# An RWKV-7 recurrence and its MLP on one core: the MLP's products as two of 64x128 in place of four of 64x64, and a planner without the count of instruction blocks

## The chip, the core and the metric

The kernel runs on one core of a Trainium2 chip. The metric is the device time of one execution in microseconds (us). A core has a matrix engine (TensorE; its matmuls are PE in the profile and its weight loads PEld), a vector engine (VectorE, DVE), a scalar engine (ScalarE, ACT), GpSimd (POOL) and a queue engine that starts DMAs here (SyncE, SP). Products are written to PSUM, from which ACT or DVE copies them to SBUF.

## The reference

Two blocks follow each other. The first is a recurrence over 768 time steps for 4 batches of 8 heads of 40 channels; the second is an MLP on the 3072 rows that come out of it.

```python
for t in range(S):                          # S = 768
    y[:, :, t] = einsum('bhd,bhde->bhe', r_t, state)
    Sa = einsum('bhde,bhe->bhd', state, a_t)
    state = state * w_t[:, :, None, :] - einsum('bhd,bhe->bhde', Sa, b_t)
    state = state + einsum('bhd,bhe->bhde', v_t, k_t)
x = y.transpose(0, 2, 1, 3).reshape(3072, 320)
h = x @ w_in                                # 320 x 2048
g = h * (1 / (1 + exp(-1.702 * h)))
out = g @ w_out                             # 2048 x 320
```

## The kernel before

The recurrence is computed in chunks of 64 time steps. There are 12 chunks; a chunk is two units (a pair of batches each), so there are 24 units. For each unit, products of 64 by 64 build the matrices that couple the steps of a chunk (prep, with the tiles ps_turn, ps_N, ps_A, ps_Av and ps_RV), six levels of doubling solve the triangular system (level, line 592, tile ps_level, each level in two halves b), the state goes on to the next chunk (update, ps_Z), and the output of the unit is read, scaled and turned (read, decayed, bridge: ps_y, y, x, ps_xT). All operands are 32-bit floats. TensorE runs each such product as two passes, each a weight load and a matmul. Four products run side by side on the four 64x64 quarters of the array: HALF chooses the rows or columns 0 to 63 or 64 to 127, and QUARTERS (line 191) lists the four combinations.

The MLP of a chunk j takes xT(j), 256 rows with the 320 channels in 5 slices of 64 for each of two row halves. `up` (line 731) makes ps_up for each of 8 blocks m of 256 hidden columns, in 5 parts, one for each slice k; ACT applies the gelu and writes g. `down` (line 748) makes ps_down for each of two halves p of the rows in 8 parts, each with two hidden slices f; ACT and DVE add the two PSUM banks into ob, and SP stores it. In both, r chooses the half of the rows of the array (the contraction) and the PSUM bank.

What order the instructions have is decided by a list scheduler in the kernel itself (Plan, line 56). Every task has a rank, a cost on each engine that can run it, what it reads and writes, the slots of each buffer, and possibly a pair of PSUM banks. There are four such pairs; tasks with `most=2` (the MLP's) may together hold two of them, and begin a new one only when two are clear. Recurrence tasks of unit i have ranks around 10 i, the conversion of the weights from 64-bit floats has ranks from 5000, and the MLP from 10000, so an MLP part is taken when nothing of a lower rank is ready. `order` goes through time: it takes for a free engine the first ready task by rank. The instructions of each engine are then issued in that order, and an engine runs them in order.

Buffers have a fixed number of slots: four for xT, ten for g, three for W (the levels' matrices). The bridge of chunk c writes xT(c) and so must come after up(c-4). Two of xT's slots hold raw weights at first.

The planner also counts TensorE's instructions. `pe` (line 225) gives a task its TensorE time and its number of instructions, 16 for each four products. `order` keeps how many were issued and when the present block of 256 began; `fetched` (line 112) lets a block begin no sooner than 3750 ns after the one before. Where the first ready TensorE task would so be held more than 100 ns, another ready one that would not be is taken in its place, if there is one:

```python
if took and e == "PE" and wait(took) > 100.0:
    took = next((t for t in able if e in t.engines and fits(t) and wait(t) <= 100.0), took)
```

Of the kernel before, what the change touches and what calls it, by code (L numbers as in the profile page):

```python
# [47 lines left out]

class Task:
    def __init__(self, rank, engines, fn, pair, most, size):  # L50
        self.instr = engines.pop("instr", 0)
        self.rank, self.engines, self.fn, self.pair, self.most, self.size = rank, engines, fn, pair, most, size
        self.after, self.then = set(), []


class Plan:

    BLOCK, FETCH = 256, 3750.0
    DELAY = {"PE": 330.0, "DVE": 130.0, "ACT": 130.0, "POOL": 150.0, "SP": 100.0}
    ISSUE = 60.0

# [27 lines left out]
    def order(self):  # L92
        for n, t in enumerate(self.tasks):
            t.n, t.left, t.ready = n, len(t.after), 0.0
            for o in t.after:
                o.then.append(t)
        free = dict.fromkeys(("PE", "ACT", "DVE", "POOL", "SP"), 0.0)
        pairs = [0.0] * self.pairs
        held, users = {}, {k: len(v) for k, v in self.of_pair.items()}
        coming = [(0.0, t.n) for t in self.tasks if not t.left]  # L100
        heapq.heapify(coming)
        able, now, wire, out, many = [], 0.0, 0.0, [], set()

        def fits(t):
            if t.pair is None or t.pair in held:
                return True
            clear = sum(p <= now for p in pairs)
            return clear > 0 if t.most is None else clear > 1 and len(many) < t.most

        issued, begun = 0, 0.0  # L110

        def fetched(t, start):

            at, left, ns, block = start, t.instr, t.engines["PE"] / t.instr, begun
            room = self.BLOCK - issued % self.BLOCK
            while left >= room:
                at += room * ns
                left -= room
                at = block = max(at, block + self.FETCH)
                room = self.BLOCK  # L120
            return at + left * ns, block

        def wait(t):
            return fetched(t, now)[0] - now - t.engines["PE"]

        while coming or able:
            while coming and coming[0][0] <= now:
                able.append(self.tasks[heapq.heappop(coming)[1]])
            able.sort(key=lambda t: (t.rank, t.n))
            took = None  # L130
            for e in free:
                if free[e] <= now:
                    took = next((t for t in able if e in t.engines and fits(t)), None)
                    if took and e == "PE" and wait(took) > 100.0:

                        took = next((t for t in able if e in t.engines and fits(t) and wait(t) <= 100.0), took)
                    if took:
                        break
            if not took:
                later = [x for x in (*free.values(), *pairs) if now < x < float("inf")]  # L140
                now = min(later + ([coming[0][0]] if coming else []))
                continue
            t = took
            able.remove(t)
            t.engine = e
            end = now + t.engines[e]
            if e == "PE":
                end, begun = fetched(t, now)
                issued += t.instr
            free[e] = end  # L150
            if e == "SP":
                wire = max(wire, now + 1500.0) + t.size / 170.0
                end = wire
            if t.pair is not None:
                if t.pair not in held:
                    held[t.pair] = next(i for i, p in enumerate(pairs) if p <= now)
                    pairs[held[t.pair]] = float("inf")
                    if t.most is not None:
                        many.add(t.pair)
                t.bank = held[t.pair]  # L160
                users[t.pair] -= 1
                if not users[t.pair]:
                    many.discard(t.pair)
                    pairs[t.bank] = end + self.DELAY[e]
            for o in t.then:
                o.ready = max(o.ready, end + (0.0 if o.engines.keys() == {e} else self.DELAY[e]))
                o.left -= 1
                if not o.left:
                    heapq.heappush(coming, (o.ready, o.n))
            t.start = now  # L170
            out.append(t)
        assert len(out) == len(self.tasks)
        return out
# [3 lines left out]
def rwkv7_gelu_quick(ctx: ExitStack, tc: tile.TileContext, time_d, w_d, chan_d, w_in, w_out, out):  # L177
    nc = tc.nc
    H, D, S = 8, 40, out.shape[0] // 4
    DM = H * D  # L180
# [5 lines left out]
    NM = NF // 2  # L186
    NK = DM // 64
    LEVELS = 6
    HALF = [slice(0, 64), slice(64, 128)]
    BITS = (0, 1)  # L190
    QUARTERS = [(0, 0), (1, 1), (0, 1), (1, 0)]
# [11 lines left out]
    def single(name, shape):  # L203
        return const.tile(shape, FP32, tag=name, name=name)

    def buf(name, n, shape, dt=FP32):

        if (name, n) not in tiles:
            s = n % plan.slots[name]
            tiles[name, n] = work.tile(shape, dt, tag=f"{name}{s}", name=name)  # L210
        return tiles[name, n]

    def psum(t, name):
        if t.pair not in psums:
            psums[t.pair] = banks.tile([128, 2, 512], FP32, tag=f"pair{t.bank}", name=name)
        return psums[t.pair]
# [7 lines left out]

    def pe(*sets):

        return {"PE": sum(n * 2 * max(58.0, cols / 1.2 + 3) for n, cols in sets), "instr": sum(16 * n for n, _ in sets)}

    def dve(n):
        return {"DVE": 170.0 + 1.03 * n}  # L230
# [1 line left out]
    def act(n):  # L232
        return {"ACT": 210.0 + 0.76 * n}
# [62 lines left out]
    w_in_sb = single("w_in_sb", [128, NK, NM, 128])  # L296
# [431 lines left out]
    g_of = lambda n: buf("g", n, [128, 2, 256])  # L728
    ob_of = lambda n: buf("ob", n, [128, DM])

    def up(j):
        for m in range(NM):
            n = j * NM + m

            def part(k, m=m):
                def go(t):
                    ph = psum(t, "ps_up")
                    for r, h in QUARTERS:
                        nc.tensor.matmul(ph[HALF[h], r, :256], w_in_sb[HALF[r], k, m, h * 64:(h + 1) * 64],  # L739
                                         xT_of(j)[HALF[r], k, :], start=k == 0, stop=k == NK - 1)  # L740
                return go
            for k in range(NK):
                plan.add(10000 + 100 * j + m, pe((1, 256)), part(k), reads=[("xT", j), ("w_in", (m // 2, k))], room=[("g", n)],
                         pair=("up", n), most=2)
            plan.add(10000 + 100 * j + m, act(512), lambda t, n=n: nc.scalar.activation(  # L745
                g_of(n), psum(t, "")[:, :, :256], ACT.Gelu_apprx_sigmoid), writes=[("g", n)], pair=("up", n))

    def down(j):
        for p in range(2):
            n = 2 * j + p  # L750

            def part(m, p=p, n=n):
                def go(t):
                    po = psum(t, "ps_down")
                    for f in (2 * m, 2 * m + 1):
                        for r, b in QUARTERS:
                            o = p * 128 + b * 64
                            nc.tensor.matmul(po[HALF[b], r, :DM], g_of(j * NM + m)[HALF[r], f % 2, o:o + 64],  # L758
                                             w_out_sb[HALF[r], f, :], start=f == 0, stop=f == NF - 1)
                return go  # L760
            for m in range(NM):
                plan.add(10000 + 100 * j + 20 * (p + 1) + m, pe((2, 320)), part(m),
                         reads=[("g", j * NM + m), ("w_out", 2 * m), ("w_out", 2 * m + 1)], pair=("down", n), most=2)

            def one(t, n=n):
                copy(t.engine)(ob_of(n), psum(t, "")[:, 0, :DM])  # L766

            def both(t, n=n):
                nc.vector.tensor_add(ob_of(n), ob_of(n), psum(t, "")[:, 1, :DM])  # L769

            def store(t, n=n, p=p):
                for b in BITS:
                    o = (2 * p + b) * S + j * C
                    nc.sync.dma_start(out[o:o + C, :], ob_of(n)[HALF[b]])
            plan.add(10000 + 100 * j, any2(320), one, writes=[("ob", n)], pair=("down", n))
            plan.add(10000 + 100 * j, dve(320), both, reads=[("ob", n)], writes=[("out", n)], pair=("down", n))
            plan.add(-100, {"SP": 120.0}, store, reads=[("ob", n), ("out", n)], size=128 * DM * 4)
# [77 lines left out]
```

## Time and profile before

| what | us |
|---|---|
| median of three runs | 1111.91 |
| lowest and highest run | 1109.09, 1114.43 |
| the profiled execution, whole | 1109.09 |
| the profiled execution, its span in the trace | 1107.4 |
| TensorE matmuls, busy | 912.8 |
| of it ps_level, all forms (L219) | 353.5 |
| of it ps_up (L739) | 251.7 |
| of it ps_down (L758) | 232.8 |
| ACT busy | 366.4 |
| DVE busy | 319.1 |

The page cuts the span into 40 slices; each digit is the busy share of an engine in tenths (9 is 90% or more):

```profile
PE   7566787756887777987768988688988999999998
DVE  4686666322423224123132131320231200000000
ACT  4333433443335333243342344333244221111211
PEclk8998989999999999999999999999999999999999
```

A slice is 27.7 us. The clock that the throttle granted to TensorE is near full throughout (mean 0.978). Weight loads overlap the matmuls. Busy times of matmuls overlap too where products run side by side; a group's busy time is the time in which at least one of its members runs.

### The profile page before, as it was taken

How to read it: one execution, taken by the hardware profiler on the slowest of the kernel's cores; microseconds unless marked ns; L12 is line 12 of the kernel's file. 1: busy time of each engine (PE TensorE's matmuls, PEld its weight loads, DVE VectorE, ACT ScalarE, POOL GpSimd, SP SyncE). 2: the span in 40 equal slices, each digit the busy share in tenths (PEclk: the TensorE clock that was granted, in tenths of full speed). 3: DMA queues.
4: the chain of work that ended last, by engine and by line, in shares of the span. 5: the costliest groups of instructions: out<-in, count | busy, mean ns of one | idle time of the engine just before them, and what ended most of it. 6: DMA issues, size and time to landing. Idle time of an engine off the chain costs nothing.

```text
span 1107.4 us, 67140 instructions
## 1 busy us (share of the span) xinstructions
PE 912.8 (82%) x32416; PEld 754.1 (68%) x32416; DVE 319.1 (29%) x688; ACT 366.4 (33%) x663; POOL 81.5 (7%) x115
## 2 busy tenths in 40 slices
PE   7566787756887777987768988688988999999998
PEld 6556676656676666777667867677877866666664
DVE  4686666322423224123132131320231200000000
ACT  4333433443335333243342344333244221111211
POOL 3322322100000000000010010000010000000000
PEclk8998989999999999999999999999999999999999
DMA  6333433201211011011111111201100000000000
GB/s 204 109 105 85 134 105 95 65 4 53 70 54 54 21 53 65 27 48 59 53 46 35 47 59 34 65 17 40 58 4 10 4 14 14 14 8 8 15 14 13
DMA packets 22542, 54.89 MB, mean 50 GB/s; under 512 B 2816, under 2 KB 14080, under 8 KB 22272
## 3 DMA queue, kind: packets, MB, share of 16 engines
q1 hardware_dynamic: 22272, 50.61, 14.8%
q8 instruction: 253, 4.15, 1.6%
q14 instruction: 17, 0.14, 0.0%
HBM read 46.66 MB, written 3.93 MB: 46 GB/s over the span
## 4 chain that ended last, share of the span: by engine, by line
PE 79%; issue 16%; DVE 2%; ACT 1%; DMA 0%; POOL 0%; SPq 0%; DVEq 0%; POOLq 0%; ACTq 0%
PE ps_up L739 19%; PE ps_down L758 19%; PE ps_level L219 18%; PE ps_turn L219 3%; PE ps_cum L219 2%; PE ps_y L219 2%; PE ps_N L219 2%; PE ps_Z L219 2%; PE ps_xT L219 1%; PE ps_saT L219 1%; PE ps_RV L219 1%; PE ps_Av L219 1%; PE ps_M L219 1%; PE ps_A L219 1%; PE ps_rz L219 1%
## 5 line engine op out<-in xcount | busy, mean ns | idle before, releaser
L219 PE MATMUL ps_level<-W 64*64 64x64 f32 (+2 forms) x8448 | 232.3, 236 | 61.3 <-issue 56.5
L219 PEld LDWEIGHTS ps_level<-W 64*64 64x64 f32 x8448 | 215.5, 137 | 77.4 <-issue 65.6
L739 PE MATMUL ps_up<-xT,w_in_sb 64*64 64x256 f32 x3840 | 251.7, 382 | 19.3 <-issue 17.2
L758 PE MATMUL ps_down<-w_out_sb,g 64*64 64x320 f32 x3072 | 232.8, 433 | 4.3 <-issue 4.1
L613 ACT COPY W<-ps_level 128x672 f32<-128x672 f32 (+1 forms) x220 | 148.7, 684 | 220.7 <-PE ps_level L219 214.2
L739 PEld LDWEIGHTS ps_up<-xT,w_in_sb 64*64 64x64 f32 x3840 | 160.5, 135 | 68.4 <-issue 28.6
L758 PEld LDWEIGHTS ps_down<-w_out_sb,g 64*64 64x64 f32 x3072 | 129.8, 134 | 70.4 <-issue 10.1
L219 PE MATMUL ps_level<-W,ident 64*64 64x80 f32 x2304 | 121.2, 238 | 8.2 <-issue 8.2
L745 ACT ACTIVATE g<-ps_up 128x512 f32<-128x512 f32 x96 | 57.4, 598 | 127.4 <-PE ps_up L739 126.4
L219 PEld LDWEIGHTS ps_level<-W,ident 64*64 64x64 f32 x2304 | 87.6, 138 | 10.2 <-issue 10.2
L769 DVE TENSOR_TENSOR ob<-ob,ps_down 128x320 f32<-128x320 f32 x24 | 11.7, 488 | 211.0 <-ACT ob L766 211.0
L766 ACT COPY ob<-ps_down 128x320 f32<-128x320 f32 x24 | 10.2, 426 | 127.5 <-PE ps_down L758 127.5
L330 POOL TENSOR_SCALAR scale<-scale 128x256 f32<-128x256 f32 (+1 forms) x36 | 41.3, 1160 | 116.0 <-DVE scale L326 116.0
L468 POOL TENSOR_TENSOR ah<-in_time,F 128x320 f32<-128x320 f32 x14 | 12.7, 904 | 360.5 <-ACT F L416 347.8
L473 POOL TENSOR_TENSOR kh<-in_time,G 128x320 f32<-128x320 f32 x18 | 16.6, 922 | 243.9 <-ACT G L414 146.2
L219 PE MATMUL ps_y<-kh,RV 64*64 64x40 f32 x768 | 28.8, 232 | 4.8 <-issue 4.8
L219 PE MATMUL ps_y<-bh,M 64*64 64x40 f32 x768 | 29.0, 235 | 4.0 <-issue 3.7
L613 DVE COPY W<-ps_level 128x416 f32<-128x416 f32 (+1 forms) x20 | 14.1, 709 | 63.1 <-PE ps_level L219 63.1
L219 PEld LDWEIGHTS ps_y<-kh,RV 64*64 64x64 f32 x768 | 27.4, 144 | 6.4 <-issue 5.2
L219 PE MATMUL ps_Z<-sa,bh 64*64 64x40 f32 x704 | 26.0, 226 | 4.1 <-issue 4.1
L219 PEld LDWEIGHTS ps_y<-bh,M 64*64 64x64 f32 x768 | 25.9, 145 | 4.6 <-issue 4.2
L508 DVE TENSOR_TENSOR W<-ps_N,upper 128x512 f32<-128x512 f32 x24 | 16.6, 691 | 42.7 <-PE ps_N L219 42.5
(113 smaller groups left out, 1111.8 us busy)
## 6 DMA issues: line engine op xcount, KB each, us to landing
in_time<-in_time SPq DMA_DIRECT2D x24, 800.0 KB, 4.6
in_chan<-in_chan SPq DMA_DIRECT2D x24, 512.0 KB, 4.3
raw<-in_w_in SPq DMA_DIRECT2D x40, 128.0 KB, 3.6
raw<-in_w_out SPq DMA_DIRECT2D x16, 320.0 KB, 3.7
in_w<-in_w SPq DMA_DIRECT2D x24, 160.0 KB, 3.4
out<-ob SPq DMA_DIRECT2D x48, 80.0 KB, 2.1
```

What stands on the lines that cost most here:

```text
L219: nc.tensor.matmul(o, lhsT, rhs, start=start, stop=True, skip_group_check=True)
L330: nc.gpsimd.tensor_scalar(scale().bitcast(FP32), scale().bitcast(FP32), low, high, ALU.max, ALU.min)
L468: plan.add(R, {"DVE": 490.0, "POOL": 900.0}, lambda t: of(t.engine).tensor_mul(ah[:, :, :D], by_head(in_time(i)[:, 3]), by_head(F_of(i))), ...
L473: plan.add(R, {"DVE": 490.0, "POOL": 900.0}, lambda t: of(t.engine).tensor_mul(kh[:, :, :D], by_head(in_time(i)[:, 0]), G()), reads=T("in_ ...
L508: plan.add(R + 1, dve(512), lambda t: nc.vector.tensor_tensor(W_of(6 * i).rearrange("p e b f n -> p e (b f) n")[:, :, :, o:o + 64], psum(t ...
L613: copy(t.engine)(W_of(s + 1)[:, :, b, :, lo:], view[:, :, :, lo:])
L739: nc.tensor.matmul(ph[HALF[h], r, :256], w_in_sb[HALF[r], k, m, h * 64:(h + 1) * 64], xT_of(j)[HALF[r], k, :], start=k == 0, stop=k == NK - 1)
L745: plan.add(10000 + 100 * j + m, act(512), lambda t, n=n: nc.scalar.activation(g_of(n), psum(t, "")[:, :, :256], ACT.Gelu_apprx_sigmoid), w ...
L758: nc.tensor.matmul(po[HALF[b], r, :DM], g_of(j * NM + m)[HALF[r], f % 2, o:o + 64], w_out_sb[HALF[r], f, :], start=f == 0, stop=f == NF - 1)
L766: copy(t.engine)(ob_of(n), psum(t, "")[:, 0, :DM])
L769: nc.vector.tensor_add(ob_of(n), ob_of(n), psum(t, "")[:, 1, :DM])
```

## The change

Two things change. The MLP's products use all 128 columns of the array at once: in `up` and `down` the loop over four quarters becomes a loop over the two row halves, with a stationary operand of 64x128 in place of 64x64, so that a part has two products of 128 output rows in place of four of 64. And the planner's count of instructions goes, with the rule that was built on it: a TensorE task takes its cost in time, and the first ready task by rank is taken.

```diff
 class Task:
     def __init__(self, rank, engines, fn, pair, most, size):
-        self.instr = engines.pop("instr", 0)
...
-    BLOCK, FETCH = 256, 3750.0
...
-        issued, begun = 0, 0.0
-
-        def fetched(t, start):
-
-            at, left, ns, block = start, t.instr, t.engines["PE"] / t.instr, begun
-            room = self.BLOCK - issued % self.BLOCK
-            while left >= room:
-                at += room * ns
-                left -= room
-                at = block = max(at, block + self.FETCH)
-                room = self.BLOCK
-            return at + left * ns, block
-
-        def wait(t):
-            return fetched(t, now)[0] - now - t.engines["PE"]
...
-                    if took and e == "PE" and wait(took) > 100.0:
-
-                        took = next((t for t in able if e in t.engines and fits(t) and wait(t) <= 100.0), took)
...
             end = now + t.engines[e]
-            if e == "PE":
-                end, begun = fetched(t, now)
-                issued += t.instr
             free[e] = end
...
-        return {"PE": sum(n * 2 * max(58.0, cols / 1.2 + 3) for n, cols in sets), "instr": sum(16 * n for n, _ in sets)}
+        return {"PE": sum(n * 2 * max(58.0, cols / 1.2 + 3) for n, cols in sets)}
...
                     ph = psum(t, "ps_up")
-                    for r, h in QUARTERS:
-                        nc.tensor.matmul(ph[HALF[h], r, :256], w_in_sb[HALF[r], k, m, h * 64:(h + 1) * 64],
+                    for r in BITS:
+                        nc.tensor.matmul(ph[:, r, :256], w_in_sb[HALF[r], k, m, :],
                                          xT_of(j)[HALF[r], k, :], start=k == 0, stop=k == NK - 1)
...
                     for f in (2 * m, 2 * m + 1):
-                        for r, b in QUARTERS:
-                            o = p * 128 + b * 64
-                            nc.tensor.matmul(po[HALF[b], r, :DM], g_of(j * NM + m)[HALF[r], f % 2, o:o + 64],
+                        for r in BITS:
+                            nc.tensor.matmul(po[:, r, :DM], g_of(j * NM + m)[HALF[r], f % 2, p * 128:p * 128 + 128],
                                              w_out_sb[HALF[r], f, :], start=f == 0, stop=f == NF - 1)
```

## The prediction

> **What bounds the kernel now.** I began with the page: how busy each engine is, and the DMA queues.
>
> ```profile
> span 1107.4 us, 67140 instructions
> PE 912.8 (82%) x32416; PEld 754.1 (68%) x32416; DVE 319.1 (29%) x688; ACT 366.4 (33%) x663; POOL 81.5 (7%) x115
> ...
> q8 instruction: 253, 4.15, 1.6%
> ```
>
> TensorE is the only engine that is busy more than a third of the time. It has 32416 matmuls and as many weight loads, 64832 instructions. The queue named "instruction" moved 253 packets and 4.15 MB: one packet for 64832 / 253 = 256 TensorE instructions, 16.4 KB each. So TensorE's program is fetched in blocks of 256 while it runs. The DMA view of two stretches gives the rate:
>
> ```profile
> q8 instruction: 129, 2.11, 1.8%
> ```
>
> That is 300 to 800 us: 129 blocks in 500 us, 3.88 us a block.
>
> ```profile
> q8 instruction: 19, 0.31, 0.9%
> ```
>
> That is 950 to 1100 us: 19 blocks in 150 us, 7.9 us a block. The two stretches have different limits. The timeline of TensorE shows the second:
>
> ```profile
> 946.32 1.34 PE L219 MATMUL ps_xT<-ident,x 64*64 64x64 f32 x80
> 947.48 17.41 PE L758 MATMUL ps_down<-w_out_sb,g 64*64 64x320 f32 x256
> 964.71 17.45 PE L739 MATMUL ps_up<-xT,w_in_sb 64*64 64x256 f32 x320
> 981.98 17.41 PE L758 MATMUL ps_down<-w_out_sb,g 64*64 64x320 f32 x256
> ```
>
> The last recurrence product is ps_xT at 946 us. From there only MLP products run, back to back. I call the four products of one contraction slice, two passes each, a "set": 8 matmuls and 8 weight loads, 16 instructions. 320 matmuls of ps_up start over 17.27 us, so a set of up takes 17.27 / 40 = 0.432 us; a set of down 17.23 / 32 = 0.538. Mean over a chunk's 40 and 32 sets: 0.479 us. Here TensorE's columns are the limit, and 256 instructions take 16 x 0.479 = 7.7 us, longer than a fetch.
>
> Up to 946 us it is the other way round. A set of the recurrence with 64 columns has its passes 58 ns apart in the timeline, 0.12 us a set, so 256 such instructions need only 1.9 us of TensorE, and the block still takes 3.88. The waits agree: what TensorE's queue waits for most is "issue", time in which nothing that the profile shows holds it.
>
> ```profile
> PEld ps_level L219 <- issue: 75.7, 69, 3.3
> ...
> PE ps_level L219 <- issue: 64.7, 62, 3.2
> ```
>
> So in the mixed stretch an MLP set costs no columns but its share of a fetch, 16/256 x 3.88 = 0.243 us, if the block has TensorE time to spare; in a run of MLP alone it costs 0.479. Counted in the timeline, there are runs of 35 sets at 777 us, 12 at 864, 57 at 883, 66 at 915 and 320 at 947, 490 sets; the other 374 of 864 lie in 317 runs of one to six sets among the recurrence. The windows before and after 947 us show why the tail has that size:
>
> ```profile
> 0.00:947.00 947.00, 181.91 (x2560) 111.54 (x2560) 38.04 (x64) 0.97 0.18 56
> 947.00:1108.00 161.00, 69.79 (x1280) 48.96 (x1280) 19.33 (x33) 1.00 0.06 12
> ```
>
> These are the matmuls of ps_up: 2560 of 3840, exactly 8 chunks of 12, before the end of the recurrence. xT has four slots, so the bridge of chunk 11 must wait for up of chunk 7. The tail of four chunks comes from that, not from the planner's rules.
>
> The sum for before: the recurrence has 64832 - 13824 = 51008 instructions, 199.3 blocks, 773 us; 374 mixed sets 91 us; 490 sets in runs 235 us. That is 1099, and 8 us are left for the start and for slow blocks.
>
> **The Trainium skill.** "Runtime: NRT & Kernel Launch", section "Instruction fetch mechanics", says that instructions come in 16 KiB blocks of 256 and that crossing a block is mostly hidden. The block size agrees with the queue's packets; the hiding doesn't: 3.88 us a block here, where TensorE has 1.9 to 2.8 us of work. "TensorE: Matmul & The Clock Gate", section "LDWEIGHTS (loading the stationary operand)", prices a load by its columns, columns / 1.2 ns. The trace agrees in slope: the shortest load of 40 columns is 109 ns and of 64 columns 129, 0.83 ns a column. "TensorEngine Tiling (Array Packing)", section "Key Properties", says that a change of the tiling mode drains TensorE. No row of before shows it: every tile there is 64 rows by at most 64 columns.
>
> **The change part by part.**
>
> 1. Two products of 64x128 in place of four of 64x64. A set goes from 16 to 8 instructions: 6912 fewer, 57920 in all, 226 blocks. Columns streamed in a pass stay 256 or 320, in two row halves that still run side by side, and the two halves write different PSUM banks as before. So a set in a run should still take 0.432 or 0.538 us. The load is the doubt: 129 + 64 x 0.83 = 182 ns by the slope above (an estimate), still under the 216 ns of a pass of up. It is hidden. If it were not, the bound is up's passes at 182 + 58 = 240 ns: 960 passes x 24 ns = 23 us. I take 0 and keep 23 for the range. ACT and DVE keep their instructions: the same 128x512 gelu, the same 128x320 copies.
>
> 2. A mixed set now costs 8/256 x 3.88 = 0.121 us. With today's order that is 374 x 0.122 = 46 us less, to 1062. The 490 sets in runs gain nothing, since fetch is not their limit.
>
> 3. The planner no longer knows of the fetch. Today, when the recurrence task on top would cross a block's end and wait over 100 ns, it takes another that doesn't; that is what puts MLP sets among the recurrence, about two a block. After, an MLP part (rank 10000 and up) is taken only when TensorE is free and no recurrence task is ready in the planner's time, in which the recurrence runs at 0.12 us a set, twice as fast as on the chip. The sets not placed so don't vanish: the xT limit forces them out later, in runs in which no recurrence is ready, at 0.479 us. A set that goes from the mix to a run costs 0.479 - 0.121 = 0.358 us. So, with n mixed sets, span = 773 + 8 + 0.121 n + 0.479 (864 - n) = 1195 - 0.358 n, and equality with before is at n = 246.
>
> 4. How large is n? Recurrence for one unit is some 17 us of TensorE by the planner's costs (410 us / 24). Its chain: a level step is 0.73 us of products, 0.33 delay, 0.72 for the ACT copy, 0.13 delay, 1.91 us, in which the two halves use 1.46 of TensorE. That leaves 0.45 us a step, 2.7 us a unit, for others, and the next unit's preparation and the previous one's read-out (9 us) rank ahead of the MLP. More gaps come from four PSUM pairs, of which the MLP may hold two, and from the exponentials' session, nearly 7 us of ACT a chunk. Against that, MLP parts can't be cut: a gap of 0.1 us takes a part of 0.43 or 1.08 us. MLP is available from the second or third chunk, for about 19 units. I bound n by 100 (2.5 us a unit: the step gaps alone) and 374 (as now) and take 230: 12 sets or 5.8 us a unit, a quarter of the planner's TensorE time. Span 1195 - 82 = 1113.
>
> 5. Changes of tile shape. Each MLP run among the recurrence is a change there and back. If each drains: a matmul of up lasts 376 ns and the next pass starts 216 after it, so 160 ns of drain, plus an unhidden load of 182 or 133: about 0.64 us for both. At 1.2 sets a run, 230 sets are 190 runs, 120 us, in 150 blocks or more: 0.8 us a block, beside 1.9 + 0.7 us of work, in 3.88. Most hides behind the fetch; where two runs share a block it doesn't. I take 12 us, bounds 0 (no drain, or all hidden) and 45.
>
> 6. The weights' conversion (DVE, rank 5000) finishes later in the order of the recurrence, since the planner's recurrence is faster; the xT slots it borrows hold up the bridge of chunk 2. On the chip TensorE is slower than planned, which covers it. 0, bound 30.
>
> Sum: 1113 + 12 = 1125 us of span. The profiled execution took 1109.09 beside its span of 1107.4, so 1126.5; it is the fastest of three (median 1111.91), so against the median about 3 us more would be natural. I say 1127.
>
> **Rivals.**
> A, the forecast: the order loses more than the halved fetch brings, 1100 to 1165. For it: the fetch rule visibly puts two sets in each block, and nothing else in the planner would. Against it: n is counted by hand.
> B, not slower: the gaps of the planner's own schedule suffice, n = 340 to 374 or more, because parts are long and PSUM pairs are scarce; with 5 us of drain 1067 to 1080, say 1072. It decides above n = 280. For it: fetch is the bound for 85% of the span, and 27 blocks go.
> C: n between 246 and 280; the two sides cancel, 1105 to 1117.
> D: a 64x128 pass is dearer than thought: load exposed (+23) and drains shown in full (+45 over A's 12) on top of A, about 1180. Against it: 8 ns of load a pass would have to show.
> E: the change doesn't do what it says: the wider product becomes four passes and the count stays 64832. Then a mixed set costs 0.243 as now: 773 + 8 + 56 + 304 = 1141, with 12 for the shapes about 1153. Nothing speaks for it.
>
> **How the numbers follow.** A 0.50, B 0.29, C 0.11, D 0.07, E 0.03. About 0.5% (5.6 us) is what can be told from no change. Slower: A's part above 1117.5 (0.46), D, E and 0.03 of C: 0.59. Faster: B, and 0.04 of A and C under 1106: 0.33. Same: 0.08. Range 1068 to 1168: it takes in B, C and most of A; D and the ends of A and B are left out. A's own range is 1100 to 1165.
>
> **What would show it.** Right: some 226 fetched blocks; passes of ps_up still 216 ns apart in the tail; the span from the last ps_xT to the end still near 160 us; runs of 30 sets and more from the middle of the recurrence on. The count of mixed sets decides between A and B. Wrong: a tail with passes above 220 ns (D), 253 blocks (E), or MLP spread evenly, with few runs before the last one (B).

## The result and the profile after

The changed kernel takes 1124.72 us (median of 4 runs, 1123.99 to 1125.89), the kernel before in the same comparison 1113.17 (1109.09 to 1115.2). The ratio is 1.0109, 95% interval 1.0077 to 1.0142: 1.1% slower. The forecast was 1127.

From the page of the changed kernel, the same lines as of the kernel before:

```profile
span 1123.9 us, 60239 instructions
PE 944.5 (84%) x28960; PEld 788.3 (70%) x28960; DVE 332.3 (30%) x699; ACT 351.0 (31%) x648; POOL 81.2 (7%) x117
...
q8 instruction: 226, 3.70, 1.4%
```

TensorE has 57920 instructions, 6912 fewer, in 226 blocks. So 27 fetches are gone, and the span is still 16.5 us longer. The timeline of TensorE at the end of the recurrence begins the tail, the stretch in which only the MLP runs:

```profile
963.91 17.50 PE L732 MATMUL ps_down<-w_out_sb,g 64*128 64x320 f32 x128
981.25 17.43 PE L714 MATMUL ps_up<-xT,w_in_sb 64*128 64x256 f32 x160
998.51 1.78 PE L732 MATMUL ps_down<-w_out_sb,g 64*128 64x320 f32 x12
```

The tail is the old one: a chunk's up starts over 17.26 us (981.25 to 998.51) with half the matmuls, so a set costs 0.432 us as before, and the tail lasts 160 us. All the difference lies before it, as the recurrence ends at 964 us and not at 947. The tile view of ps_up says the same of the load (after the position come the shortest, the median and the longest, in ns):

```profile
L714 PEld LDWEIGHTS ps_up<-xT,w_in_sb x1920: 182/187/333, 274.0 to 1101.6; 64*128 64x128 f32 x192
L714 PE MATMUL ps_up<-xT,w_in_sb x1920: 376/376/790, 274.0 to 1101.8; 64*128 64x256 f32 x192
```

182 ns is what the slope of the shorter loads gave, and the matmul is as long as before. The two windows, before and after the last recurrence product, for ps_up alone:

```profile
0.00:964.00 964.00, 158.07 (x1280) 121.83 (x1280) 38.22 (x64) 0.97 0.18 55
964.00:1124.00 160.00, 69.73 (x640) 61.97 (x640) 19.11 (x32) 1.00 0.05 11
```

1280 of 1920 is two thirds again, 8 chunks of 12. The four slots of xT forbid a longer tail than four chunks, and both kernels leave as much for it as the slots allow. What is new is where the MLP sits before it. The timeline at 522 us, the middle of the recurrence:

```profile
521.93 0.30 PE L194 MATMUL ps_Z<-sa,bh 64*64 64x40 f32 x8
522.05 0.30 PE L194 MATMUL ps_Z<-in_time,kh 64*64 64x40 f32 x8
522.16 0.30 PE L194 MATMUL ps_Z<-sa,bh 64*64 64x40 f32 x8
522.40 3.50 PE L732 MATMUL ps_down<-w_out_sb,g 64*128 64x320 f32 x24
525.73 17.43 PE L714 MATMUL ps_up<-xT,w_in_sb 64*128 64x256 f32 x160
543.10 1.40 PE L194 MATMUL ps_xT<-ident,x 64*64 64x64 f32 x80
```

Nothing of the recurrence could be taken in the plan, so 46 MLP sets run alone for 21 us, and the first thing after them is the bridge (ps_xT) that had waited for them. Counted in the timeline, such runs hold 46 sets at 522 us, 28 at 616, 700 and 787, 31 at 870, 62 at 896, 68 at 930 and 320 in the tail: 611 sets, where the kernel before had 490. The other 253 (before 374), the mixed sets, lie among the recurrence, in 122 runs that mostly are one or two sets.

The MLP also starts later. The tile view of w_out_sb, the converted weights of down, in the kernel before and in the changed one:

```profile
L343 DVE SCALAR_TENSOR_TENSOR w_out_sb<-w_out_sb,scale x16: 491/492/1029, 115.5 to 192.6; 128x320 f32<-128x320 f32 x16
```

```profile
L318 DVE SCALAR_TENSOR_TENSOR w_out_sb<-w_out_sb,scale x16: 491/492/493, 209.7 to 332.3; 128x320 f32<-128x320 f32 x16
```

The last conversion begins at 332 us where it began at 193, the first product of up at 274 and not 121, the first of down at 474 and not 278. Counted up to 515 us, just before the first long run, the changed kernel has issued 60 MLP sets and the kernel before 151. So 91 of the 121 mixed sets that are missing are missing there.

### The profile page after: what moved, and what is told of

It reads as the page before. It is cut to its first block, busy times and chain, and to the rows that moved or that the text cites. A ratio compares the mean times of both kernels' runs of the same rounds, so it can differ in the third digit from the quotient of the medians.

```text
span 1123.9 us, 60239 instructions
## 1 busy us (share of the span) xinstructions
PE 944.5 (84%) x28960; PEld 788.3 (70%) x28960; DVE 332.3 (30%) x699; ACT 351.0 (31%) x648; POOL 81.2 (7%) x117
## 4 chain that ended last, share of the span: by engine, by line
PE 82%; issue 15%; DVE 1%; ACT 1%; POOL 0%; POOLq 0%; DVEq 0%; ACTq 0%
PE ps_down L732 20%; PE ps_up L714 20%; PE ps_level L194 19%; PE ps_turn L194 4%; PE ps_y L194 2%; PE ps_N L194 2%; PE ps_cum L194 2%; PE ps_Z L194 2%; PE ps_xT L194 1%; PE ps_A L194 1%; PE ps_M L194 1%; PE ps_saT L194 1%; PE ps_Av L194 1%; PE ps_ahZ L194 1%; PE ps_RV L194 1%
## 5 line engine op out<-in xcount | busy, mean ns | idle before, releaser
L194 PEld LDWEIGHTS ps_level<-W 64*64 64x64 f32 x8448 | 198.1, 139 | 86.3 <-issue 74.4
L732 PE MATMUL ps_down<-w_out_sb,g 64*128 64x320 f32 x1536 | 229.1, 441 | 2.0 <-issue 1.9
L714 PE MATMUL ps_up<-xT,w_in_sb 64*128 64x256 f32 x1920 | 227.8, 387 | 0.5 <-ACT g L720 0.5
L588 ACT COPY W<-ps_level 128x672 f32<-128x672 f32 (+1 forms) x206 | 137.7, 678 | 211.9 <-PE ps_level L194 204.9
L714 PEld LDWEIGHTS ps_up<-xT,w_in_sb 64*128 64x128 f32 x1920 | 183.8, 190 | 25.9 <-ACT g L720 0.8
L732 PEld LDWEIGHTS ps_down<-w_out_sb,g 64*128 64x128 f32 x1536 | 143.2, 187 | 53.7 <-issue 2.8
L194 PEld LDWEIGHTS ps_level<-W,ident 64*64 64x64 f32 x2304 | 79.2, 140 | 13.3 <-issue 13.3
L588 DVE COPY W<-ps_level 128x672 f32<-128x672 f32 (+1 forms) x34 | 26.3, 786 | 74.5 <-PE ps_level L194 66.9
L698 DVE COPY xT<-ps_xT 128x640 f32<-128x640 f32 x10 | 8.2, 825 | 116.1 <-PE ps_xT L194 116.1
L634 ACT COPY saT<-ps_saT 128x512 f32<-128x512 f32 x23 | 13.5, 585 | 68.0 <-PE ps_saT L194 67.9
```

The source lines that it names most:

```text
L194: nc.tensor.matmul(o, lhsT, rhs, start=start, stop=True, skip_group_check=True)
L588: copy(t.engine)(W_of(s + 1)[:, :, b, :, lo:], view[:, :, :, lo:])
L634: plan.add(R + 6, any2(512), lambda t: copy(t.engine)(saT_of(i).rearrange("p (r j) t -> p r (j t)", r=2), psum(t, "")[:, :, :256]), writes ...
L698: plan.add(R + 6, any2(640), lambda t: copy(t.engine)(xT_of(c).rearrange("p k (q b t) -> p q b k t", q=2, b=2)[:, p], psum(t, "")[:, :, :N ...
L714: nc.tensor.matmul(ph[:, r, :256], w_in_sb[HALF[r], k, m, :], xT_of(j)[HALF[r], k, :], start=k == 0, stop=k == NK - 1)
L732: nc.tensor.matmul(po[:, r, :DM], g_of(j * NM + m)[HALF[r], f % 2, p * 128:p * 128 + 128], w_out_sb[HALF[r], f, :], start=f == 0, stop=f = ...
```

## The experiments

I set two readings against each other. S: the order without the count of blocks costs what the sum says, and the halved fetch brings its full 0.122 us for each mixed set, since changes of tile shape hide behind the fetch. D: the changes of shape don't hide and eat what the fetch saves. Edits are cut to their main lines. Runs of one group below stood on one chip; the kernel before was timed beside them, 1092 to 1099 us on these chips.

**e3: the new products in the old order.** The kernel before with only the loops over `BITS`; the planner still counts 16.

```diff
-                    for r, h in QUARTERS:
-                        nc.tensor.matmul(ph[HALF[h], r, :256], w_in_sb[HALF[r], k, m, h * 64:(h + 1) * 64],
+                    for r in BITS:
+                        nc.tensor.matmul(ph[:, r, :256], w_in_sb[HALF[r], k, m, :],
...
```

> The 64x128 products in exactly the order of the kernel before (the planner still counts 16 instructions for an MLP set). Step 2 of the prediction and theory S: 374 x 0.122 = 46 us less, 1062 of span, ratio 0.955 to 0.965. Theory D: changes of shape at every MLP run among the recurrence, some 160 at 0.43 us, 69 us, of which a part hides behind the fetch: 1085 to 1105, ratio 0.98 to 1.0.

Measured: 1089.01 us beside 1092.34, ratio 0.9974 (0.9952 to 0.9996). This is 3 us of the 46 that S expected; D's band holds it.

**e2: the old products in the new order.** The changed kernel with the four 64x64 products back.

```diff
-                    for r in BITS:
-                        nc.tensor.matmul(ph[:, r, :256], w_in_sb[HALF[r], k, m, :],
+                    for r, h in QUARTERS:
+                        nc.tensor.matmul(ph[HALF[h], r, :256], w_in_sb[HALF[r], k, m, h * 64:(h + 1) * 64],
...
```

> The changed kernel with the 64x64 products back, so the same order without the planner's count. By the prediction's sum with the 253 mixed sets that the changed kernel shows: 773 + 8 + 0.243 x 253 + 0.479 x 611 = 1135 of span, ratio to before 1.02 to 1.03, and 31 us more than the changed kernel would be without any cost of shape changes (1104), 11 more than it is (1124). Theory S: 1135, as the order alone costs 28 us. Theory D: 1120 to 1128, no different from the changed kernel, if the changes of shape eat all that the halved fetch brings.

Measured: 1111.38 us beside 1092.34, ratio 1.0192 (1.017 to 1.0214). D's spans, divided by the 1107.4 of the kernel before, are ratios of 1.011 to 1.019, and S's band begins at 1.02: the interval touches both, so this run doesn't decide between them. It does show that the order alone makes the kernel slower. Since the changed kernel had been measured on another chip, I ran both together later (e8, e9, below).

**e1: the new products, with the planner's count kept and right.**

```diff
-    def pe(*sets):
+    def pe(*sets, per=16):
-        return {"PE": ..., "instr": sum(16 * n for n, _ in sets)}
+        return {"PE": ..., "instr": sum(per * n for n, _ in sets)}
...
-                plan.add(10000 + 100 * j + m, pe((1, 256)), part(k), ...
+                plan.add(10000 + 100 * j + m, pe((1, 256), per=8), part(k), ...
```

> The kernel before with the 64x128 products, and the planner's count kept and set right (8 instructions for an MLP set, 16 for a recurrence set). Theory S (the order costs, the halved fetch brings its full 0.122 us a mixed set): at least as many mixed sets as before (374), so 1062 or less of span and a ratio to before of 0.93 to 0.965. Theory D (each change of tile shape takes about 0.43 us of TensorE, 0.15 going in and 0.36 coming out against some 0.08 before, and that eats most of the fetch saved): 1085 to 1107, ratio 0.98 to 1.0.

Measured: 1082.33 us, ratio 0.9924 (0.9896 to 0.9951). It has 416 mixed sets in 150 runs, more than any kernel so far, and gains 10 us, in D's band and far from S's.

To see where the saving of e3 goes, I counted each block of 256 TensorE instructions between 220 and 940 us by the time that its MLP sets need, in the traces of before and e3:

```
MLP in the block   before: blocks, mean us, sets rec. + MLP  e3: blocks, mean us, sets rec. + MLP
none               51   3.81   16.0 + 0.0                    50   3.54   16.0 + 0.0
under 1.0 us       43   3.74   14.3 + 1.7                    31   3.45   15.2 + 1.5
1.0 to 1.6 us      38   3.59   13.6 + 2.4                    38   3.85   14.7 + 2.5
1.6 to 2.2 us      21   3.95   11.8 + 4.2                    18   4.65   13.9 + 4.2
```

Some 25 blocks of each trace with more MLP than that are left out. Where a block begins in the trace is an assumption, and other beginnings move the means by up to 0.2 us; the two traces come from two chips besides. Up to 1.6 us of MLP a block takes about as long as one of recurrence alone: there the fetch is the limit. With four sets that is over in e3. There such a block holds two recurrence sets more than before and nearly three changes of shape (1.3 pairs), and takes 0.7 us longer; in e8 against e9, one order on one chip, it is 4.6 us against 3.9. So two things can take the saving back: the changes, and blocks that are now full of work, since 256 instructions hold more of it.

**e7: the price of a change of shape by itself.** Slices 1 and 3 of up's five as four 64x64 products, so that TensorE changes shape in its tail, where it is the limit.

```diff
-                    for r in BITS:
-                        nc.tensor.matmul(ph[:, r, :256], w_in_sb[HALF[r], k, m, :],
+                    for r, o in product(BITS, [HALF, [slice(0, 128)]][k % 2 == 0]):
+                        nc.tensor.matmul(ph[o, r, :256], w_in_sb[HALF[r], k, m, o],
```

> The changed kernel with slices 1 and 3 of the five in up as four 64x64 products, 0, 2 and 4 as two of 64x128: two pairs of shape changes for each block of hidden columns, 16 a chunk, where TensorE is the limit and nothing hides them. The tail of four chunks takes 160 us without them. Theory S (changes cost nothing): 160. Theory D at 0.43 us a pair: 64 x 0.43 = 27 us more, 187; at 0.21 us, what the gaps between starts in the trace of the changed kernel suggest beyond a normal pass, 173.

Measured: 1170.61 us, one run. The timeline of its tail:

```profile
1002.97 23.22 PE L714 MATMUL ps_up<-xT,w_in_sb 64*128 64x256 f32 x224
1026.02 17.39 PE L732 MATMUL ps_down<-w_out_sb,g 64*128 64x320 f32 x128
1043.25 16.82 PE L714 MATMUL ps_up<-xT,w_in_sb 64*128 64x256 f32 x164
```

A chunk's up now takes 1026.02 - 1002.97 = 23.05 us from its first start to that of the next group, where it was 17.26; down, which has one shape, is unchanged at 17.23. 16 pairs of changes cost 5.79 us, 0.36 us a pair. All four groups of up in the tail take 23.05 us, each with 16 pairs, and the tail lasts 183 us. So D's 0.43 us was somewhat high, 0.21 too low, and S's nothing is excluded.

**e6: is it the fetch that binds the recurrence?** Most of the MLP's products are left out.

```diff
-            for k in range(NK):
+            for k in range(1):
...
-            for m in range(NM):
+            for m in range(1):
...
```

> The changed kernel with most of the MLP's products left out (up makes one slice of five, down one part of eight: 144 sets of 864). What remains is 51008 instructions of the recurrence and 1152 of the MLP, 204 blocks. If the fetch binds the recurrence: 204 x 3.7 to 3.85 = 755 to 785, and some 25 for the products after its end, 780 to 810. If its own chain through ACT and DVE binds it: the 3.8 us a block would be an accident of the MLP's presence, and the time falls to 550 to 650, near the planner's own time without a fetch.

```profile
PE 595.0 (72%) x26080; PEld 518.6 (63%) x26080; DVE 335.7 (41%) x700; ACT 343.8 (42%) x643; POOL 86.9 (11%) x121
...
q8 instruction: 204, 3.34, 1.6%
...
PE 66%; issue 25%; ACT 3%; DVE 3%; DMA 2%; SPq 0%; POOL 0%; ACTq 0%; DVEq 0%; POOLq 0%
```

Those are three lines of its page; the last has the shares of the chain that ended last. One run took 826.49 us, its span is 824.8. The last ps_xT is at 784 us, after 202 blocks, 3.88 us each, just as with the MLP among them (3.88). The span is over the band, since the products after the recurrence took 40 us and not 25.

The time alone would also fit a recurrence that is bound by its own chain. Two things speak against that. ACT and DVE hold 6% of the chain that ended last, and "issue" 25%. And the pauses of TensorE follow the fetch. Between 220 and 780 us there are 109 pauses of over 0.8 us, in which no matmul or load starts; 106 of them end 2.0 to 3.2 us after a packet of the instruction queue began, while these packets are 3.8 us apart on average. In the kernel before it is 83 of 84. So the recurrence waits for its fetch.

**e4 and e5: all blocks filled.** A rule in the planner that looks at the slack in a block, and not only at its end, with the new products (e4) and the old ones (e5).

```diff
-                    if took and e == "PE" and wait(took) > 100.0:
-                        took = next((t for t in able if e in t.engines and fits(t) and wait(t) <= 100.0), took)
+                    if took and e == "PE" and took.most is None:
+                        room = self.BLOCK - issued % self.BLOCK
+                        spare = begun + self.FETCH - now - room * self.NS
+                        fill = next((t for t in able if e in t.engines and t.most and fits(t)), None)
+                        if fill and spare > fill.engines["PE"] + (0.0 if filling else self.SHAPE):
+                            took = fill
```

`filling` is true after an MLP part. `NS` is 7.5 in both. e4 has `FETCH` 4000, `SHAPE` 450 and the counts of e1; e5 has 3750, 0 and 16 for each set.

> 64x128 products with another rule in the planner: when a recurrence task is next and the time until the next block can begin exceeds what the rest of this block needs at 7.5 ns an instruction, an MLP part that fits in that slack is taken first (the first one of a run must leave 450 ns more). All but some 70 MLP sets then lie among the recurrence, in about 210 runs. Theory S (shape changes hide, instructions are what counts): fetch 226 blocks x 3.8 = 860 and what is left at the start and the end, 950 to 985, and faster than e5. Theory D (a pair of changes costs 0.43 us): 90 us of changes on top of some 800 us of TensorE's own work, which no longer hide, and the first 200 us without MLP: 1000 to 1035, slower than e5.

> The kernel before (64x64 products, 16 instructions a set) with the rule of e4, without its 450 ns as nothing changes shape. By the prediction's sum with some 790 mixed sets: 773 + 8 + 0.243 x 790 + 0.479 x 74 = 1008; the fetch alone is 253 blocks x 3.8 = 961. Theory D: 985 to 1015, ratio 0.90 to 0.93, faster than e4 in spite of 27 more blocks. Theory S: the same time for this kernel, but slower than e4. If the recurrence is not bound by the fetch but by its own chain of waits, no gain: the MLP pieces would delay it, 1090 or more.

Measured: e4 1024.64 us, ratio 0.9379 (0.9326 to 0.9431); e5 1017.05, ratio 0.9318 (0.9278 to 0.9358), both beside 1093.25. The page of e5:

```profile
span 1014.3 us, 67105 instructions
...
PE   6758777999888899899898898998988989989998
...
q8 instruction: 253, 4.15, 1.7%
```

In both, 792 of 864 sets are mixed and the tail is one chunk, with the same four slots of xT: the slots alone didn't make the tail of four chunks. The spans, 1021 and 1014 us, lie in D's bands. e5 fetches 27 blocks more than e4 and takes 7.6 us less by the medians; the intervals of the ratios overlap, and their `FETCH` differs too, so what is clear is only that halving the instructions gained nothing where nearly every block is filled. The sum of the prediction, with n = 790, gave 1008 for e5, whose span is 1014. Both are 6 to 7% faster than the kernel before beside them.

**e8 and e9: the changed kernel and e2's on one chip, five rounds.**

> The changed kernel itself, to stand on one chip beside e9. With 0.36 us a pair of shape changes (e7) and 129 runs among the recurrence, the changes cost up to 46 us, the fetch saved by 253 mixed sets is 31 us, and part of the changes hides: ratio to before 1.005 to 1.02.

> The same order with 64x64 products (the kernel of e2), on the chip of e8. If the wide products bring a net gain in this order, e9 is slower than e8 by 0.3 to 1.2% (the two earlier ratios, 1.019 and 1.011, came from different chips); if the changes of shape take all of it, the two agree within 0.3%.

Measured: 1112.12 us, ratio 1.012 (1.0086 to 1.0155), for the changed kernel; 1112.26, ratio 1.0128 (1.0089 to 1.0166), for the same order with the old products. They agree, though the intervals would hide a difference of some 0.5%. The ratio of e2's kernel was 1.0192 on the first chip and is 1.0128 on this one, so ratios from two chips can't be subtracted to 0.5%.

These two traces show where the saved fetch goes. Up to the tail (951.5 us in e8, 950.6 in e9) I added up the pauses of TensorE of over 0.4 us, in which no matmul or load starts:

| | e9, 64x64 | e8, 64x128 |
|---|---|---|
| up to the tail, us | 950.6 | 951.5 |
| of it pauses | 239.3 | 193.6 |
| the rest, TensorE at work or in shorter waits | 711.3 | 757.9 |

The pauses shrink by 46 us (by 43 if only those of over 0.8 us count), and the rest grows by 47. The 129 MLP runs before the tail are as many pairs of changes, and at the 0.36 us of e7 they come to 46 us. So with fewer fetches TensorE does wait less, and the changes of shape are about as long as what it waits less. How much of the changes fell into former pauses, and how much of the fetch's saving was never there, this sum of one trace each doesn't tell.

## Why the prediction came out

The forecast was 1127 us and 1124.72 came, but two errors cancelled, and that is luck. The bound was named rightly for the kernel before: two stretches, fetch up to the end of the recurrence (e6 and the pauses) and TensorE's columns after it. Step by step:

1. The products: 226 blocks, passes of 216 ns, loads of 182 ns that hide in the tail. As said; rival D's exposed load and rival E fall with it.
2. The halved fetch, 0.122 us for each mixed set and 46 us in the old order: no such gain of time. e3 gained 3 us, and between e9 and e8 the pauses shrank while TensorE's own time grew as much. The step holds only where the block has TensorE time to spare, a condition that the prediction stated and then used as met everywhere; with the wide products four sets a block and their changes use the time up.
3. and 4. The order: 253 mixed sets against the 230 taken, and forced runs of 28 to 68 sets at the bridges, as described. The direction is shown by e9 and e2: the order alone costs 1.3 to 1.9%, 14 to 21 us. By the sum, 121 sets moved from a mixed 0.243 to 0.479 should cost 29 us with the old products. So this term was too large. Some of the sets mixed before may not have been free; no run shows that. The 253 also lie in the band of rival C, 246 to 280: with them the sum gives 1116 of span with the 12 us for shapes, 9 us over the kernel before and not 18. The measured loss is A's all the same, since the products gave nothing against the order's cost. And that the tail of four chunks comes from xT's slots, not from the planner's rules, is wrong: e4 and e5 have the same slots, another rule and a tail of one chunk.
5. Changes of shape: 0.64 us a pair was put by argument, e7 has 0.36; 190 runs were put, 122 short ones came. The 190 rest on a misreading: in the timeline of before a run of 64x64 products is broken up where products of the recurrence start between them. e3 has the same order, and there the 374 sets lie in some 154 runs, 2.4 a run and not 1.2. 12 us were taken for what shows. In the changed kernel, 1195 - 0.358 x 253 = 1104, and 1123.9 - 1104 = 20 us stand where 12 were put, with the fuller blocks in it and the order's term, which was too large, against it. So the wrong step was that most of the changes hides behind the fetch: between e9 and e8 the wide products gain nothing that can be seen.
6. The weights' conversion was put at nothing. It ends 140 us later, and most of the missing mixed sets are missing in the first 515 us. How much of the order's cost is owed to the late weights, and how much to a recurrence that leaves no gaps in the plan, no run tells apart: e2 and e9 have both.

The total of 1127 came this near because two terms were off in opposite ways: the order, put at 34 us (144 sets at 0.236), cost 14 to 21, and the net of the new products is near zero, where fetch and changes were put at 28 - 12 = 16 us of gain (230 x 0.122 = 28). The forecast's direction stands on what e9 shows: the changed kernel is slower because the planner's count and rule are gone, and the new products give nothing back. Rival B fell on n: it needed over 280 mixed sets. Of rival D the exposed load fell; that the changes show was nearer to it than to the 12 us.

## What to carry to other kernels

When an instruction stream is fetched in blocks slower than it is executed, find out what each block has to spare before counting fewer instructions as time: only blocks with spare time pay. There, work that is long for its number of instructions is best put evenly into every block; in this kernel that was worth 6 to 7%, with either shape of product, while the shape alone was worth 0.3% in the old order and nothing measurable in the new. And price a change of tile shape where the engine has no slack, as e7 does, before mixing shapes.

## What the runs showed of the hardware

A pair of changes between 64x64 and 64x128 tiles costs 0.36 us at 256 columns (e7). The Trainium skill, "TensorEngine Tiling (Array Packing)", section "Key Properties", says that a change of mode drains TensorE. e7 shows that a change has a price; that it is a drain isn't shown, as the first pass after a change starts some 0.31 us after the one before it, where passes of one shape are 0.216 apart and a matmul is recorded with 0.376.

Blocks of recurrence alone took 3.81 us in the trace of before and 3.75 in e2's, but 3.67 in the changed kernel's, 3.54 in e3's and 3.45 in e1's, which have the new products. e1, e2 and e3 stood on one chip. The means differ by what stands ahead of a block: one of recurrence alone that follows another of its kind takes 3.7 to 3.8 us in all five, and the few (3 to 9 a trace) that follow a block with three or more MLP sets take 2.3 to 3.0 us in the mean in the kernels with the new products. So a fetch runs ahead while a full block executes.

The changed kernel's tail takes 160.0 us in the trace after the change and in that of e8, on another chip; the stretch before it takes 963.9 and 951.5 us. In these two traces the whole difference of the chips lies in the stretch where TensorE waits for its fetch.
